# A new order for the items of phase one in a fused attention and MoE kernel

## The chip, the core and the metric

The kernel runs on one core of a Trainium2 chip. The metric is the device time of one execution in microseconds (us). Engines are named as in the profile: PE (TensorE matmul), PEld (its weight loads), DVE (VectorE), ACT (ScalarE), POOL (GpSimd), SP (SyncE, which here only issues transfers). L949 is line 949 of the kernel.

## The reference

Attention with pooled keys and values, followed by a feed-forward layer with a periodic activation, all in f32:

```python
# q, k, v: (8 batches, 8 heads, 576, 64)
k_p = k.reshape(B, H, 72, 8, D).mean(axis=3)
v_p = v.reshape(B, H, 72, 8, D).mean(axis=3)
scores = scale * np.matmul(q, k_p.transpose(0, 1, 3, 2))
scores = scores - np.max(scores, axis=-1, keepdims=True)
attn = np.exp(scores)
attn = attn / (np.sum(attn, axis=-1, keepdims=True) + 1e-09)
attn_out = np.matmul(attn, v_p)
x = attn_out.transpose(0, 2, 1, 3).reshape(4608, 512)
# w_in (512, 2048), w_out (2048, 512)
h = x @ w_in
s = np.sin(alpha * h)
g = h + s * s / (alpha + 1e-09)
out = g @ w_out
```

## The kernel before

**Two phases.** Phase one (to about 513 us) makes attention, `x @ w_in` and the activation, and stores g to a DRAM tensor, `g_bridge`. Phase two (`outputs`, matmuls of L1294) reads g back and multiplies by `w_out`. The change touches phase one only.

**Units and groups.** The tokens are cut into nine units of 512 and w_in into four column blocks, so that phase one has 36 groups, n = 4u + J (unit u, block J, here called group 0 to 3 of a unit). Each group makes a 2 x 2 block product with seven products in place of eight, `M1` to `M7`, of four matmuls each (`M5.2` is part 2 of the fifth, all of them L975). They need sums of blocks of x: `sums_of_x` (L939, items `sn`, `sx`) makes four of them per unit on DVE. In units 1 to 6 some products (5 and 1) are again split in seven smaller ones, with items `i.a`, `i.b`, `i.d`, `i.e` (matmuls, L1066) and the small copies and the add between them, `i.ca` (L1079), `i.cm`, `i.cb` and `i.ad` (L1089). These need sums made by `inner_x` (each unit) and `inner_w_in` (`w2_1`, `w2_5`; once, in unit 0), L931 on POOL.

**One group behind the products.** ACT and DVE bring the results from PSUM to the tile of g: `c16`, `p5`, `c67` are copies (L950), `a00`, `a01`, `a11`, `f10` DVE adds with a PSUM operand and `f1` one of SBUF tiles alone (all L949), `s` and `q` sine and square on ACT (L1044, L1051). `st` stores the tile of g with two transfers on SP's queue (L1099). The tile is called `h`; two buffers of it serve all groups in turn, so that the first write into a tile (the `a00` of a group) waits for the stores of the group two before. PSUM has eight banks: 0, 1, 2 and one of 3 and 4 in turn hold a group's accumulators; scores and `values` borrow from these and 5 to 7.

**Attention of the next batch.** In unit u, attention of batch u + 1 runs between the products: `scores`, the row maxima and their subtraction (`shift`), `exp`, `norm` (POOL, L496), `turn` (transposition on DVE) and `move` (transfers on SP), `values` (PE), and `out` (copies to x). Beside it the next inputs are loaded: `load_k`, `load_q`, `load_v` (six transfers on SP: two of L280, four of L285), pooled on POOL by `pool_k`, `pool_vm`, `pool_v`. `turn_q` turns q: `qa`, `qb`, `qc` on DVE, then `qd` and `qe` with eight transfers each on SP (L370).

**The order.** All these items stand in one agenda, each with a key; `perform` emits them in the order of the keys, and each engine keeps the order in which its instructions are emitted. A group adds 7 n to its keys, a unit 28 u:

```python
where = ORDER[self.kind(n)]
for m, f in acts.items():
    if m in where:
        self.at(7 * n + where[m], f)
```

`ORDER` (L42) is a table of such keys written out by hand: `U` for the attention items of units 1 to 6, `U0` for those of unit 0, `first0` to `first3` for the groups of unit 0, `enter` for the first group of unit 1, `mid0` to `mid3` for those of the units between, `exit` and `end0` to `end3` for the last ones. `F`, `U7` and `R` hold the start, unit 7's sums and later loads. Semaphores between engines follow from the tiles that an item reads and writes, so a new key changes what an instruction stands behind, never what it needs.

Of the kernel before, what the change touches and what calls it, by code (L numbers as in the profile page):

```python
# [43 lines left out]
    "load_k0": -3.59252, "load_v": -0.96965, "scores0": 3.279, "shift1": 6.66681, "shift0": 7.14828, "scores1": 7.66855, "shift2": 7.69635,  # L44
    "exp1": 11.39419, "exp0": 11.40344, "shift3": 11.6083, "exp2": 11.66391, "exp3": 11.68798, "norm0": 11.85811, "norm1": 11.86021, "norm2": 11.9294,
    "norm3": 11.93036, "pool_k0": 11.93266, "pool_v": 11.93269, "pool_vm": 11.9327, "turn2": 12.15533, "turn1": 12.33183, "turn3": 12.34767,
    "load_q": 13.4176, "load_k1": 13.54022, "turn0": 15.964, "move": 24.04575, "clean": 24.12855, "qa": 24.12869, "values": 24.12873,
    "out4": 24.12875, "qb": 24.12884, "pool_k1": 24.12885, "out0": 24.12885, "mark": 24.12895, "qc": 24.129, "out2": 24.129, "sx0": 24.1291,
    "inner_x": 24.12915, "out3": 24.33175, "k_t": 24.4364, "k_c": 24.4956, "qd": 24.83712, "out1": 24.87145, "sx1": 24.87995, "qe": 24.96216,
    "sx2": 25.5786, "sx3": 33.62096},  # L50
# [12 lines left out]
    "vsum": 1.50081, "qrest": 1.50141, "ahead": 1.502, "load_v": 2.08618, "pq0": 2.15962, "win3": 2.42169, "vals": 2.503, "sx2": 2.50351,  # L63
    "sx3": 2.50375, "score4": 2.504, "pq3": 2.82144, "win2": 2.94801, "pq4": 4.05233, "pq2": 4.0566, "pq1": 4.07221, "qt0": 4.511, "qt1": 4.51172,
    "kt0": 4.51227, "kc0": 4.96887, "scores0": 5.518, "shift0": 5.52, "shift1": 5.521, "comb1": 7.38091, "qt3": 7.92628, "qt2": 8.13953,
    "pool_vm": 8.75569, "qt4": 9.526, "exp1": 9.52613, "exp0": 9.52662, "scores1": 10.519, "shift2": 10.522, "norm0": 12.96627, "shift3": 13.00319,
    "comb2": 13.15659, "norm1": 13.38469, "turn0": 13.38824, "exp2": 14.22682, "exp3": 15.56789, "exp4": 15.57472, "load_k0": 16.01154,
    "load_q": 16.43872, "norm2": 16.65626, "load_k1": 16.66341, "norm3": 16.67159, "comb3a": 16.67343, "turn1": 16.69456, "comb3b": 16.77826,
    "turn3": 17.03674, "turn2": 17.289, "nrest": 17.37323, "move1": 18.86855, "move2": 18.96992, "clean": 18.98312, "move0": 19.548, "arest": 21.5955,
    "qc": 21.89678, "pool_v": 22.64595, "w2_1": 22.78383, "pool_k1": 22.83011, "pool_k0": 22.88021, "qa": 23.561, "qb": 23.562, "qd": 23.84216,  # L70
    "vrest": 26.13943, "values": 26.551, "qe": 26.565, "out0": 26.7312, "out2": 26.9598, "mark": 26.9713, "w2_5": 27.34755, "sn0": 27.5,
    "inner_x": 27.55453, "out1": 27.76959, "out4": 27.8955, "out3": 27.97572, "kt1": 28.19418, "sn2": 28.3493, "sn1": 28.40019, "kc1": 28.50762,
    "sn3": 28.51},
# [7 lines left out]
    "M1.2": -2.57294, "M1.0": -2.53472, "M1.1": -2.45741, "M1.3": -2.25355, "c16": -1.1367, "M5.0": -0.09345, "M5.1": 0.9728, "M2.0": 1.17425,  # L81
    "M6.0": 1.17485, "M2.1": 1.21724, "M6.2": 1.21765, "M5.2": 1.21779, "M6.1": 1.21784, "M6.3": 1.21789, "M5.3": 1.21819, "M2.2": 1.21845,
    "c67": 2.29615, "M2.3": 2.3555, "M7.0": 2.35565, "p5": 2.384, "s00": 2.38414, "q00": 2.3842, "M7.1": 2.5708, "M7.2": 2.57295, "M3.2": 3.16644,
    "M3.0": 3.47531, "M3.1": 3.63665, "M7.3": 3.7191, "M3.3": 4.06192, "a00": 6.599, "a11": 6.59915, "M4.0": 6.82409, "a01": 6.89334, "M4.1": 7.01225,
    "M4.2": 7.0125, "s11": 7.04685, "s01": 7.11736, "M4.3": 7.14095, "s10": 7.149, "q1": 7.19287, "q01": 7.22535, "f10": 8.3468, "f1": 8.63666,
    "st": 10.05},
"end1": {
    "M5.0": -3.33019, "M5.1": -2.72125, "M1.0": -0.17668, "M5.2": -0.17606, "M1.1": -0.17602, "M1.2": -0.06105, "M1.3": -0.0, "M5.3": 0.01245,
    "c16": 0.08171, "M6.1": 0.14395, "M6.0": 0.15524, "M6.2": 0.1611, "p5": 0.19815, "M6.3": 0.2009, "M2.1": 0.2077, "c67": 0.20789, "M2.2": 0.20881,
    "M2.3": 0.20922, "M2.0": 0.20955, "s00": 0.3, "q00": 0.3002, "a00": 2.19325, "M7.1": 2.79825, "M3.0": 2.80473, "M7.0": 2.81351, "M7.3": 2.88245,  # L90
    "M7.2": 2.88791, "M3.1": 2.88955, "M3.2": 2.9988, "M3.3": 3.21335, "a11": 3.46515, "s11": 4.32131, "M4.0": 4.4354, "a01": 5.1294, "M4.1": 7.91733,
    "M4.2": 7.92785, "M4.3": 7.99325, "s10": 8.1665, "q1": 8.17037, "s01": 8.2013, "q01": 8.36455, "f10": 9.25247, "f1": 9.6345, "st": 10.05},
"end2": {
    "M5.0": -5.21769, "M5.1": -4.19849, "M1.0": -3.17899, "M1.1": -2.75025, "M1.2": -2.51525, "M1.3": 0.90215, "M5.2": 0.99395, "M5.3": 0.99415,
    "c16": 1.14695, "p5": 1.1828, "M6.0": 1.4299, "M2.0": 1.4318, "M6.2": 1.43214, "M2.1": 1.43255, "M2.2": 1.5857, "M6.1": 1.71475, "M6.3": 1.7193,
    "M2.3": 1.7196, "c67": 1.78765, "s00": 1.78813, "q00": 1.79224, "M7.1": 2.3807, "M3.0": 2.38083, "M7.0": 2.38084, "M7.2": 2.38085, "M7.3": 2.3819,
    "a00": 2.69669, "a11": 2.7835, "M3.1": 3.71335, "M3.2": 3.93591, "M3.3": 5.35825, "M4.0": 5.57345, "a01": 5.76695, "M4.3": 6.28487,
    "M4.1": 6.46705, "M4.2": 7.97136, "s11": 9.31248, "s10": 9.36555, "q1": 9.36695, "s01": 9.43775, "q01": 9.4416, "f1": 9.6118, "f10": 9.90706,
    "st": 10.05},
"end3": {  # L100
    "M5.0": -5.29345, "M5.1": -4.88305, "M1.2": -2.23625, "M1.0": -1.54834, "M1.3": -1.48014, "M5.2": -1.2153, "M1.1": -1.21312, "c16": 2.27975,
    "M6.2": 2.3529, "M6.0": 2.35688, "M6.1": 2.35962, "M2.1": 2.36295, "M2.0": 2.3654, "M6.3": 2.3726, "c67": 2.37425, "M2.2": 2.4012,
    "M5.3": 2.40185, "M7.1": 2.41368, "M7.0": 2.41595, "M2.3": 2.4234, "p5": 2.48725, "M3.0": 2.51711, "M7.3": 2.5939, "M7.2": 2.61123, "a11": 2.612,
    "M3.1": 2.6266, "M3.2": 2.68157, "s00": 2.7151, "M3.3": 2.76182, "q00": 2.82195, "s11": 2.9428, "a01": 3.3439, "a00": 3.60325, "M4.1": 3.9026,
    "M4.2": 4.2433, "M4.0": 4.41961, "M4.3": 4.42479, "s01": 4.63625, "s10": 4.64555, "q01": 6.26891, "q1": 6.5869, "f1": 6.76776, "f10": 7.38579,
    "st": 10.05},
"enter": {
    "M1.0": -0.5012, "M1.2": -0.49378, "M1.1": -0.48667, "M1.3": -0.47146, "M5.0": -0.45225, "M5.1": -0.39509, "M5.2": -0.11055, "M5.3": -0.01999,
    "c16": 0.2794, "p5": 0.86945, "M6.0": 2.04465, "M2.0": 2.65792, "M2.1": 4.32577, "M2.3": 4.65506, "M6.1": 4.856, "M6.3": 4.86001, "M6.2": 4.87325,
    "M2.2": 6.26441, "c67": 7.13695, "s00": 7.13705, "q00": 7.13865, "a00": 9.0381, "M3.1": 9.2872, "M7.0": 10.26028, "M3.2": 11.00189,  # L110
    "M7.2": 11.0438, "M7.1": 11.12859, "M3.3": 11.34036, "M3.0": 11.34068, "M7.3": 11.41202, "a01": 11.61553, "a11": 11.72873, "M4.3": 11.78194,
    "M4.2": 11.92945, "s01": 11.93326, "s11": 11.9409, "M4.1": 11.9883, "M4.0": 12.04209, "s10": 12.24896, "q01": 12.24962, "q1": 13.17745,
    "f1": 13.21186, "f10": 13.40255, "st": 15.95645},
"exit": {
    "i.a": -5.02158, "i.ca": -4.768, "i.cm": -4.76115, "i.b": -4.15145, "i.cb": -3.5502, "i.d": -3.09985, "i.ad": -3.09835, "i.e1": -2.6215,
    "i.e5": -2.5921, "c16": -1.98745, "M6.3": -1.6521, "M6.1": 1.03682, "M2.1": 1.99737, "M6.2": 2.6094, "M2.0": 2.6097, "M6.0": 2.61059,
    "M2.2": 2.6107, "p5": 2.70895, "c67": 3.12873, "M2.3": 3.15565, "s00": 3.1652, "q00": 3.19285, "M3.1": 3.1934, "M7.0": 3.21229, "M3.0": 3.57143,
    "M7.3": 3.57944, "M7.1": 3.61026, "M7.2": 3.66851, "M3.3": 3.6861, "a00": 3.72485, "M3.2": 3.742, "a11": 3.8399, "a01": 4.32695, "M4.1": 4.53493,
    "M4.0": 4.5453, "M4.3": 4.82867, "M4.2": 4.96155, "s11": 5.86985, "s01": 5.87902, "s10": 5.9176, "q1": 6.17963, "q01": 6.2042, "f1": 6.79974,
    "f10": 7.5896, "st": 9.38135},  # L120
"first0": {
    "M1.0": 1.50081, "M1.3": 1.5013, "M1.2": 1.50138, "M1.1": 1.5016, "c16": 1.50164, "M5.2": 1.85931, "M5.3": 2.00457, "M5.0": 2.1577,
# [1448 lines left out]
```

## Time and profile before

| what | value |
|---|---|
| median of 3 runs | 905.83 us (905.42 to 906.15) |
| profiled execution, its span | 902.2 us |
| PE busy | 894.0 us, 99% |
| DVE busy | 678.2 us, 75% |
| ACT busy | 457.3 us, 51% |
| POOL busy | 206.5 us, 23% |
| granted PE clock, all slices | 9 of tenths (9 is 90% or more) |
| phase one, phase two | 0 to about 513 us, 513 to 902 us |

The profiled execution's own time is the span, 902.2 us; 3.6 us of the median lie around it. One unit takes 54.7 us, with the boundaries at about 86, 140.7, 195.4, 250.1, 304.8, 359.5 and 414.2 us. By such stretches the busy times are (us, with counts of instructions; then the granted clock, the share of the DMA engines and GB/s):

```profile
195.40:250.10 54.70, 54.70 (x470) 46.85 (x470) 37.85 (x65) 43.06 (x97) 23.40 (x29) 1.00 0.68 194
250.10:304.80 54.70, 54.70 (x471) 46.98 (x470) 38.01 (x65) 43.12 (x97) 23.56 (x29) 1.00 0.68 194
```

The columns after the stretch are its length, then PE, PEld, DVE, ACT and POOL. PE counts as busy through the whole of such a unit, while the other engines have from a fifth to more than a half of the time to spare.

### The profile page before, as it was taken

Reading aid. Unit: us, or ns where it says so; the run is one execution under the profiler, and the core shown is the slowest. Engines: PE = TensorE matmul, PEld = TensorE weight load, DVE = VectorE, ACT = ScalarE, POOL = GpSimd, SP = SyncE. Lnnn points to the kernel's source line nnn. Section 1 sums busy time; section 2 is a strip of 40 time slices with the busy share of each in tenths; the row PEclk is TensorE's granted clock in tenths of the full one; section 3 lists DMA queues with packets and bytes.
Section 4 is the critical chain, followed back from the end, with each engine's and each line's share of the span. In section 5 each row is a group of like instructions: output and inputs, shape, how many; then the busy total and the mean of one; then the engine's idle time right before and its main releaser. Section 6 shows DMA issues by size and latency. Waiting matters only on the chain.

```text
span 902.2 us, 18350 instructions
## 1 busy us (share of the span) xinstructions
PE 894.0 (99%) x7146; PEld 815.0 (90%) x7146; DVE 678.2 (75%) x1016; ACT 457.3 (51%) x1073; POOL 206.5 (23%) x235
## 2 busy tenths in 40 slices
PE   8999999999999999999999999999999999999997
PEld 5787888978888898888888899999999999999997
DVE  7576857668586684854466999979798888889894
ACT  5696878868787787786885611211111111111111
POOL 4969561814418164130000000000000000000000
PEclk9999999999999999999999999999999999999999
DMA  9956766666766666645426346261618172534401
GB/s 271 229 170 181 209 193 177 209 173 200 212 179 197 198 187 173 175 133 200 181 104 213 99 152 193 65 191 35 224 30 231 31 201 63 171 92 130 134 15 40
DMA packets 128751, 141.17 MB, mean 156 GB/s; under 512 B 46920, under 2 KB 95704, under 8 KB 128664
## 3 DMA queue, kind: packets, MB, share of 16 engines
q1 hardware_dynamic: 125880, 137.88, 52.6%
q10 hardware_dynamic: 2784, 2.11, 0.9%
q8 instruction: 57, 0.93, 0.4%
q14 instruction: 30, 0.25, 0.1%
HBM read 75.37 MB, written 47.19 MB: 136 GB/s over the span
## 4 chain that ended last, share of the span: by engine, by line
PE 98%; DVE 1%; DMA 0%; ACT 0%; issue 0%; ACTq 0%
PE PS L1294 43%; PE PS L975 41%; PE PS L1066 7%; PE PS L444 2%; PE PS L739 2%; PE PS L752 1%; DVE home L939 1%; DMA q<-in_q_dram 0%; PE PS L553 0%; PE PS L532 0%; PE PS L1131 0%; PE PS L416 0%; PE PS L697 0%; PE PS L343 0%; PE PS L695 0%; PE PS L607 0%
## 5 line engine op out<-in xcount | busy, mean ns | idle before, releaser
L975 PE MATMUL PS<-home,a 128*128 128x256 f32 x968 | 250.3, 382 | 0.0
L975 PEld LDWEIGHTS PS<-home,a 128*128 128x128 f32 x968 | 177.3, 190 | 28.6 <-issue 4.7
L975 PE MATMUL PS<-home,as 128*128 128x256 f32 x728 | 194.9, 381 | 0.9 <-DVE home L939 0.9
L975 PEld LDWEIGHTS PS<-home,as 128*128 128x128 f32 x728 | 134.1, 190 | 18.3 <-DVE home L939 0.9
L1294 PE MATMUL PS<-s,wb 128*128 128x144 f32 x896 | 119.1, 286 | 0.0
L1294 PEld LDWEIGHTS PS<-s,wb 128*128 128x128 f32 x896 | 113.6, 190 | 0.0
L1051 ACT ACTIVATE s<-s,c 128x256 f32<-128x256 f32 (+1 forms) x216 | 112.7, 580 | 0.0
L1344 POOL TENSOR_TENSOR cc<-cc,cb 128x576 f32<-128x576 f32 x1 | 2.0, 1974 | 483.1 <-DVE cb L1249 483.1
L949 DVE TENSOR_TENSOR h<-PS,s 128x512 f32<-128x512 f32 x72 | 49.5, 687 | 70.3 <-ACT s L1051 70.3
L1430 ACT COPY PS<-PS 128x144 f32<-128x144 f32 x56 | 14.7, 263 | 143.4 <-PE PS L1294 140.8
L1294 PE MATMUL PS<-r,wb 128*128 128x144 f32 x512 | 73.2, 286 | 0.0
L1294 PE MATMUL PS<-s,a 128*128 128x144 f32 x512 | 73.2, 286 | 0.0
L1044 ACT ACTIVATE s<-h,al 128x256 f32<-128x256 f32 x144 | 64.1, 502 | 16.4 <-DVE h L949 13.3
L271 POOL TENSOR_TENSOR kvin<-kvin 96x768 f32<-96x768 f32 (+3 forms) x42 | 69.9, 1665 | 3.1 <-DMA a<-in_moe_w_in_dram 0.6
L1294 PEld LDWEIGHTS PS<-r,wb 128*128 128x128 f32 x512 | 67.1, 190 | 0.1
L1294 PEld LDWEIGHTS PS<-s,a 128*128 128x128 f32 x512 | 67.1, 190 | 0.0
L949 DVE TENSOR_TENSOR h<-PS,p 128x512 f32<-128x512 f32 x72 | 49.1, 685 | 22.3 <-PE PS L975 21.7
L950 ACT COPY PS<-PS 128x512 f32<-128x512 f32 x72 | 41.4, 576 | 46.2 <-PE PS L975 23.0
L1044 ACT ACTIVATE s<-PS,al 128x256 f32<-128x256 f32 x144 | 60.3, 473 | 6.1 <-PE PS L975 5.8
L498 POOL TENSOR_TENSOR ex<-ex,sm 128x576 f32<-128x576 f32 (+1 forms) x28 | 35.2, 1270 | 109.8 <-DVE sm L497 108.9
L1412 ACT COPY PS<-PS 128x144 f32<-128x144 f32 x56 | 14.7, 263 | 88.7 <-PE PS L1294 88.7
L949 DVE TENSOR_TENSOR h<-h,s 128x1024 f32<-128x1024 f32 x36 | 44.8, 1246 | 14.2 <-ACT s L1051 14.1
(217 smaller groups left out, 1531.4 us busy)
## 6 DMA issues: line engine op xcount, KB each, us to landing
g_bridge<-h SPq DMA_DIRECT2D x72, 512.0 KB
r<-g_bridge SPq DMA_DIRECT2D x31, 1152.0 KB
out_dram<-o SPq DMA_DIRECT2D x122, 72.0 KB
kvin<-in_k_dram SPq DMA_DIRECT2D x14, 576.0 KB
q<-in_q_dram SPq DMA_DIRECT2D x7, 1024.0 KB
kvin<-in_v_dram SPq DMA_DIRECT2D x14, 512.0 KB
ex<-tr SPq DMA_DIRECT2D x54, 92.0 KB
ex<-tr SPq DMA_DIRECT2D x54, 88.0 KB
```

Of the source, the lines that this page charges most:

```text
L271: self.nc.gpsimd.tensor_tensor(out=t[..., 0:w] if w > D else out, in0=t[..., 0:w], in1=t[..., w:2 * w], op=OP.add)
L444: nc.tensor.matmul(ps[e][r0 + r:r0 + r + q.shape[-1], h, :], q[s], kb[s, hp, :], start=True, stop=True)
L498: nc.gpsimd.tensor_tensor(out=E(i), in0=E(i), in1=sm.unsqueeze(2).to_broadcast([P, n, Sp]), op=OP.mult)
L739: nc.tensor.matmul(o[r:r + 64], w, x, start=start and i < 2, stop=False, skip_group_check=True)
L949: add = lambda o, x, y: nc.vector.tensor_tensor(out=o, in0=x, in1=y, op=OP.add)
L950: copy = lambda o, x: nc.scalar.copy(out=o, in_=x)
L975: nc.tensor.matmul(ps[:, jj, :], self.A[p][:, kk, f * P:(f + 1) * P], x[:, kk, :], start=start and p not in G.begun, stop=(kk == 1), skip_ ...
L1044: self.nc.scalar.activation(out=G.s()[:, i, jj, j, :], in_=src[:, jj], func=AF.Sin, scale=self.al[:, f:f + 1])
L1051: self.nc.scalar.activation(out=x, in_=x, func=AF.Square, scale=self.c[:, f:f + 1])
L1066: nc.tensor.matmul(out, W[m][:, G.J], self.X2[p][m], start=start, stop=True, skip_group_check=True)
L1294: nc.tensor.matmul(out, W[:, J // 2, J % 2, :], A[:, J, :], start=(start and J == 0), stop=(J == self.NJ - 1), skip_group_check=True)
L1412: nc.scalar.copy(out=st["x1"][:, 1, :], in_=st["x1"][:, 0, :])
```

## The change

Only keys in `ORDER` are changed: in `U`, `U0`, `first0` to `first3`, `enter`, `mid0` to `mid3`, `exit` and `end0` to `end3`. `F`, `U7` and `R` stay, and no code beside the table is edited (it moves ten lines down, so that L949 before is L959 after; lines are named by their old numbers here). Every instruction, tile and transfer is the same in both kernels; only what stands before what on each engine differs. The keys of all loads stay as they were. Items on POOL and the DVE adds that read two SBUF tiles are placed so that they lie apart.

Many keys get new values with the same neighbours as before. Those that the prediction speaks of, in unit 0 (`U0`) and in units 1 to 6 (`U`, `mid2`), with all other keys left out:

```diff
 "U": {
-    "load_k0": -3.59252, "load_v": -0.96965, ...
-    "norm0": 11.85811, ... "pool_k0": 11.93266, "pool_v": 11.93269, "pool_vm": 11.9327, ...
-    ... "move": 24.04575, "clean": 24.12855, "qa": 24.12869, "values": 24.12873,
-    ... "qb": 24.12884, "pool_k1": 24.12885, ... "qc": 24.129, ...
-    "inner_x": 24.12915, ... "qd": 24.83712, ... "sx1": 24.87995, "qe": 24.96216,
+    "load_k0": -3.59252, "load_v": -0.96965, ...
+    ... "pool_v": 11.5152928, ... "norm0": 11.816381, ... "pool_k0": 12.3504188, ...
+    ... "pool_k1": 13.7954806, "turn0": 14.2914411, "move": 16.8183036, "pool_vm": 16.8469318,
+    "clean": 22.6818447, "qc": 22.6854708, "qa": 24.0974238, "values": 24.0975073, "qb": 24.1363647, ...
+    ... "inner_x": 24.3451414, ... "sx1": 24.5126011, "qd": 24.5236839, ... "qe": 24.532439,
 "U0": {
-    ... "pool_v": 22.64595, "w2_1": 22.78383, "pool_k1": 22.83011, "pool_k0": 22.88021, ...
-    ... "mark": 26.9713, "w2_5": 27.34755, "sn0": 27.5, "inner_x": 27.55453, ...
-    ... "kt1": 28.19418, "sn2": 28.3493, "sn1": 28.40019, "kc1": 28.50762, "sn3": 28.51},
+    ... "pool_v": 16.4275201, ... "pool_k1": 16.6636208, ... "w2_1": 24.4248686, ...
+    ... "sn0": 27.3094653, ... "pool_k0": 28.2511337, "sn1": 28.2512193, "sn2": 28.2512644,
+    "kt1": 28.2512817, "kc1": 29.1202333, "w2_5": 36.7683461, "inner_x": 36.9454661, "mark": 39.3525585, "sn3": 39.8922378},
 "mid2": {
-    "i.a": -2.3038, ... "f10": 10.1286, "s01": 10.12874, "q01": 10.88815, "f1": 11.0343, "st": 11.5035},
+    "i.a": -2.3730868, ... "f10": 10.0974848, "s01": 10.1335768, "q01": 10.5326811, "f1": 10.5635624, "st": 13.6858195},
```

## The prediction

> **What bounds the kernel now.** I read the page first, then the waits of PE, then the matmul starts of phase one, and only then the other engines' timelines, at the places where the new order moves something.
>
> ```profile
> PE 894.0 (99%) x7146; PEld 815.0 (90%) x7146; DVE 678.2 (75%) x1016; ACT 457.3 (51%) x1073; POOL 206.5 (23%) x235
> ```
>
> ```profile
> PE PS L1131 <- DVE full L1463: 1.1, 1, 1.1
> PE PS L532 <- DMA q<-in_q_dram: 1.0, 1, 1.0
> PE PS L975 <- DVE home L939: 0.9, 2, 0.5
> ```
>
> PE is busy 894.0 of 902.2 us, and the longest waits listed for it come to 3.0 us, 2.1 of them at the start, which the change leaves alone. Since a busy PE may hide stalls, I took the spacing of matmul starts in the trace. An L975 matmul follows the one before after 216 ns, an L1066 one after 112 ns. From about 30 us to 513 us nearly every start keeps this pitch. What exceeds it, other than the 0.1 us at each change between large and small tiles, is 1.3 us between 84 and 91 us and, in each 54.7 us unit, two places of 0.25 us where the last inner products wait for the add of L1089. Phase two, from 513 us, has no spare start at all and is not edited. So phase one's order can give back some 3 to 4 us and no more, while it can lose any amount: PE's work is the same, and only a new wait of PE makes a time.
>
> The adds that the change is about are those of L939 (`sums_of_x`), L949 with three SBUF tiles (`f1`) and L931 on POOL. Where they meet, this is seen; the timelines of DVE and POOL, start, us, instruction:
>
> ```profile
> 85.02 4.05 DVE L939 TENSOR_TENSOR home<-home 128x512 f32<-128x512 f32 x2 [1.68 <-ACT home L666]
> 89.00 1.75 DVE L939 TENSOR_TENSOR home<-home,home 128x512 f32<-128x512 f32 x1
> 91.09 1.34 DVE L939 TENSOR_TENSOR home<-home,home 128x512 f32<-128x512 f32 x1
> ```
>
> ```profile
> 86.93 1.59 POOL L931 TENSOR_TENSOR q<-q,as 128x512 f32<-128x512 f32 x1
> ```
>
> Four adds take 7.1 us beside `w2_5` (L931); with POOL idle one takes 0.69 us (the L939 add at 191.85 us).
>
> **The change, part by part.** Both kernels issue the same instructions; the sequences on each engine differ. I compared them item by item.
>
> (a) Boundary of units 0 and 1. `w2_5` (5 to 6 us on POOL) now follows `pool_k0`, ahead of `inner_x` and `mark`, and needs nothing that is late, so it ends near 84 us, before `sn0`. The four adds then cost 4 x 0.69 = 2.8 us. On PE that is worth what PE waits there: 0.71 + 0.15 us at 87 us (M5 of group 4 waits for `sn0`) and 0.49 us after `kt1`, together 1.3 us. Against it, SP now has unit 1's `load_k0` ahead of group 1's store, and group 2's store (1.07 us of SP) ahead of the last eight q DMAs, which feed `scores0` of unit 1 at 91.92 us; the last of them is issued at 89.1 us now, so up to 0.5 us can come back. I take 0.8 us gained, with bounds of 1.3 gained and 1 lost.
>
> [...]
>
> (b) In each unit one more matmul pair stands between the last `i.d` and `i.e` products of a group, so the two waits of 0.25 us go. The second of them is spent again: one M2 pair moves behind `values`, so `values` comes 0.43 us earlier after `i.e1`, while `p5`, which frees its bank, still ends behind the same ACT items. Net 0.25 us in 6 units: 1.5 us gained (bounds 0 and 3).
>
> (c) In units, `f1` meets POOL hardly at all (1.22 us mean, 1.54 us once), and the one add that does, `sx1` (0.95 against 0.69 us), stays beside `inner_x`. I cost this at nothing: M6, which waits for it, is 8 us later.
>
> (d) POOL: `pool_v` moves ahead of the norms, `pool_k1` ahead of `pool_vm`. `pool_v` waits for the v rows, which land before 268 us where norm0's multiplication stood at 269.5 us; `pool_vm` (5.4 us) would end near 292 us, `values` begins at 297 us. Covered by 1.5 us and 5 us. If that cover were gone, PE would wait at `values`.
>
> (e) SP: this is the one I find uncovered. SP's timeline at a boundary of units:
>
> ```profile
> 253.64 1.85 SPq L370 DMA_DIRECT2D q<-tr  x3
> 255.59 1.07 SPq L1099 DMA_DIRECT2D g_bridge<-h  x2
> 256.76 2.25 SPq L280 DMA_DIRECT2D kvin<-in_v_dram  x2
> 259.05 2.69 SPq L285 DMA_DIRECT2D vr<-in_v_dram  x4
> 267.89 0.96 SPq L1099 DMA_DIRECT2D g_bridge<-h  x2
> ```
>
> Sixteen q DMAs, the two stores of group 2 (`st`), the six v loads. `load_v` keeps its key, -0.97 from the next unit's start. Group 2 starts 14 keys before that start, so `mid2`'s `st` goes from 11.50 - 14 = -2.50 to 13.69 - 14 = -0.31. So the stores now stand behind the six loads. Queued behind them on SP is only group 3's store, 8 us later. Who waits is DVE: two `h` buffers serve all groups, and `a00` of the next unit's group 0 writes the buffer that these stores read; in the new sequence it waits for just these two landings. The same place on DVE, ACT and PE:
>
> ```profile
> 262.91 0.68 DVE L949 TENSOR_TENSOR h<-PS,s 128x512 f32<-128x512 f32 x1
> ```
>
> ```profile
> 263.91 0.36 ACT L1079 COPY PS<-PS 128x256 f32<-128x256 f32 x1
> ```
>
> ```profile
> 264.57 0.39 PE L1066 MATMUL PS<-ex,aM 128*128 128x128 f32 x2
> ```
>
> `a00` at 262.91 frees bank 1, `i.ca` copies into it, and `i.b` is the next product on it. From a landing to `i.b` take 0.68 + 0.36 + 0.1 us, so PE, which I place 0.25 us earlier by (b), waits for every landing after 264.57 - 0.25 - 1.15 = 263.2 us. Now the stores land at 261.71 (the last step of their semaphore in the trace's records): 1.2 us before they are needed.
>
> When would they land? The six loads take SP from 256.76 to 261.75, 5.0 us. The q DMAs can start earlier: they wait for DVE's `qa`, `qb`, `qc`, and `qc` (0.66 us) now precedes the two and waits only for moves that landed early; `qa` need no longer follow `f10`, but `qb` still does. That brings q's start from 244.98 to about 243.25, 1.7 us. So the stores are issued 3.3 us later, at 258.9. Fastest end: group 3's stores, with nothing in the queue, land 4.8 us after issue (267.89 to 272.67), which gives 263.7 and a wait of 0.5 us. Slowest end: the queue is served in order (the moves issued at 283.04, behind a store, send their first packet at 285.29, when the store's packets end). The v data took from 259.7 to 267.4 us, 7.7 us, of which the last 2.6 us were the `vr` loads, moving on about 4 of the 16 engines (24 packets of 86 ns in 0.5 us). In the new order the v data begin 1 us after their issue at 253.9 (as k loads do), so the four engines are free at 262.6; a store's share of 32 packets of 86 ns makes 265.4, and from the last packet to the landing 2.2 us passed before (259.5 to 261.71): 267.6 and a wait of 4.4 us. I am nearer to the slow end, since the order of the queue is seen and the four engines are seen, but the 2.2 us held other traffic; I take 266.0 us, a wait of 2.8 us.
>
> It occurs at the boundaries into units 2 to 6, five times (at the first the store comes before the loads, at the last there are no loads): 5 x 2.8 = 14 us, with bounds of 2.5 and 22. Nothing takes it back: DVE, ACT and PE stand together, and what follows in the unit shifts with them.
>
> [...]
>
> Sum: 905.8 - 0.8 - 1.5 + 14 = 917.5 us. The profiled span is 902.2, the runs' median 905.83, so 3.6 us lie around the span; the terms are differences and go on the median.
>
> **The rivals.** *The stores land in time* (faster). If the v loads leave the store's engines free early enough for a landing before 263.2 us, the change is left with (a) and (b): 905.8 - 2.3 = 903.5 us, at best 901. For it speaks that the fast end is only 0.5 us late; q's start would have to come 0.5 us earlier still, or the stores land in 4.3 us. Against it, the stores of this very place took 6.1 us (255.59 to 261.71) and the queue was in order. *Nothing reaches PE*: the adds are cleared but the 1.3 us returns by the q DMAs and (b) is lost to `p5`: 905.8. For it: 99% PE. *A wait at `values` instead*: `f10` of group 2 now stands between `qa` and `qb`, and frees the bank of `values`' second part. It waits with `qa` for the 15th move to land (near 239.8 us); if that comes 1 us late, PE waits 0.8 to 1.5 us in six units, 5 to 9 us, so 909 to 912 alone. Against it, `f10` waits until 241.4 us for its square already.
>
> **How the numbers follow.** Less than 0.2% (1.8 us) is no change for this kernel. Forecast (e): 0.71. Stores in time, 903.5: 0.17. Nothing: 0.07. `values`: 0.05, slower too. So faster 0.17, same 0.07, slower 0.76. The range takes the forecast's waits of up to 3.4 us (923) and reaches down to 903.5, where the first rival lies; outside are the slow end's last part (about 0.1) and the better half of that rival. The forecast's own range is 907 to 925.
>
> **What would show it.** Right: in the timeline of SP each group-2 store behind the v loads; on DVE an L949 `h<-PS,s` after 2 to 4 us of idle time put down to a DMA, five times, and as much idle or stretched time of PE before L1066; the unit period 57 instead of 54.7 us. The adds at 85 us near 0.7 to 0.9 us each. Wrong: a period of 54.5 us, or a00 at its old place behind the shifts, or PE waiting elsewhere.

## The result, and the profile after

The changed kernel takes 925.80 us (median of 5 runs, 924.61 to 927.17), the kernel before 905.83 us (5 runs, 905.42 to 906.22). The ratio is 1.0224, with a 95% interval of 1.0211 to 1.0236: 20 us slower. The forecast was 917.5 us in a range of 903.5 to 923: the right side, with a loss 8.3 us too small, and 2.8 us outside the range. All lines of the code stand ten lower in the changed kernel (L959 is the old L949). The profiled execution has a span of 925.4 us, and its own time is 927.17: 1.8 us lie around the span, and 1.7 to 2.1 in every execution that has both numbers. Other executions of the kernel before with a span of 902.2 us took 904.0 to 904.3 us, so the one profiled there was shorter than its kernel's median by some 1.7 us; the 3.6 us given above for the time around its span are too much by as much.

The page's first part and its chain, in the places of those of before:

```profile
PE 903.8 (98%) x7146; PEld 824.3 (89%) x7146; DVE 678.7 (73%) x1016; ACT 459.5 (50%) x1073; POOL 204.3 (22%) x235
```

```profile
PE 82%; DMA 7%; SPq 4%; DVE 3%; POOL 2%; issue 1%; ACT 1%; ACTq 0%; DVEq 0%; POOLq 0%
```

PE is busy for 98% of the span (99% before), and the span is 23 us longer. Of these, 2.3 us lie ahead of the first product, which starts at 23.9 us here and at 21.6 before. This start belongs to the execution and not to the order: over all the kernels below it lies at 21.4 to 21.9 us or at 23.0 to 23.9, whichever keys they have, while phase two takes 389.0 us in nearly all of them. What makes it early or late stays open; a difference of under some 2 us between two executions can be this start alone. The chain says more than the busy share: before, 98% of it was PE; now DMA and SP's queue hold 11%. The waits of PE and, below, of DVE (engine, line, what it waited for: us in total, times, longest):

```profile
PE PS L1076 <- ACT PS L1089: 10.4, 5, 3.3
PE PS L454 <- issue: 1.2, 1, 1.2
...
PE PS L732 <- DVE h L959: 0.9, 1, 0.9
PE PS L985 <- DVE h L959: 0.9, 1, 0.9
PE PS L749 <- DVE h L959: 0.3, 1, 0.3
```

```profile
DVE h L959 <- DMA g_bridge<-h: 14.6, 5, 3.8
```

Five waits of DVE for the landing of a store of g, and behind each, five waits of PE ahead of `i.b`. This is the place that step (e) of the prediction named. The boundary that the prediction showed now looks so, on SP, DVE, ACT and PE (start, us, instruction, idle time before it):

```profile
254.34 11.40 SPq L380 DMA_DIRECT2D q<-tr  x16
265.84 1.36 SPq L290 DMA_DIRECT2D kvin<-in_v_dram  x2
267.25 2.70 SPq L295 DMA_DIRECT2D vr<-in_v_dram  x4
270.06 0.90 SPq L1109 DMA_DIRECT2D g_bridge<-h  x2
```

```profile
278.37 0.69 DVE L959 TENSOR_TENSOR h<-PS,s 128x512 f32<-128x512 f32 x1 [2.41 <-DMA g_bridge<-h]
```

```profile
279.15 0.36 ACT L1089 COPY PS<-PS 128x256 f32<-128x256 f32 x1 [2.29 <-DVE h L959]
```

```profile
277.11 0.59 PE L985 MATMUL PS<-home,as 128*128 128x256 f32 x2
279.56 0.49 PE L1076 MATMUL PS<-ex,aM 128*128 128x128 f32 x2 [1.86 <-ACT PS L1089]
```

The second store is issued at 270.49 us and lands at 278.25 by its semaphore's records; `a00` starts 0.12 us later, and `i.b` 1.3 us after the landing.

**Where the 20 us are.** The pitch of a kind of matmul is the usual time from one start to the next (216 ns for L985). I added up by how much starts of matmuls exceed it, from the first product to the end of phase one, wherever it is over 0.15 us: 38.7 us after, 17.6 before (13.4 us of the latter and 15.3 of the former lie at `values`, where some starts lie far apart even without a wait: at 297.5 to 300.4 us of the kernel before by 371 to 374 ns at L739 and by 513 to 518 ns at L752). The 21.1 us between them, in this one execution: 11.2 us at the five `i.b`; 3.8 us of slow matmuls behind three of these; 1.9 us more at `values` of units 1 to 6 (15.3 against 13.4); 1.6 us more at the boundary of units 0 and 1 (5.4 against 3.8), where the granted clock is 0.50 from 86.07 to 89.48 us; 1.4 us inside the scores of unit 3, which the profile puts down to nothing that it shows ("issue"); 1.1 us at 60 us. The 3.8 us are seen in windows around the same wait (stretch, length, then busy us and instructions of PE, PEld, DVE, ACT, POOL, then PE's granted clock, DMA share, GB/s):

```profile
277.70:279.50 1.80, 0.01 (x1) 0.00 (x0) 1.13 (x2) 0.35 (x1) 0.46 (x1) 1.00 0.01 3
279.50:280.50 1.00, 0.94 (x6) 0.91 (x7) 0.97 (x2) 0.14 (x2) 0.00 (x0) 1.00 0.00 0
280.50:281.50 1.00, 1.00 (x4) 0.79 (x4) 1.00 (x2) 1.00 (x4) 0.00 (x0) 0.57 0.00 0
281.50:282.50 1.00, 1.00 (x5) 0.90 (x4) 0.67 (x3) 1.00 (x2) 0.00 (x0) 0.50 0.00 0
282.50:283.50 1.00, 1.00 (x4) 0.72 (x3) 1.00 (x1) 0.26 (x1) 0.00 (x0) 0.50 0.02 8
283.50:284.50 1.00, 1.00 (x6) 0.88 (x5) 0.97 (x4) 0.00 (x0) 0.00 (x0) 0.73 0.00 0
```

At 280.63 us, 1.1 us after PE is at work again, its clock falls to 0.5 for 3.41 us, and matmuls of L985 follow one another after 427 ns in place of 216.

### The profile page after: what moved, and what is told of

Read it like the earlier page. It is cut to its first block, busy times and chain, and to the rows that moved or that the text cites. A ratio compares the mean times of both kernels' runs of the same rounds, so it can differ in the third digit from the quotient of the medians.

```text
span 925.4 us, 18368 instructions
## 1 busy us (share of the span) xinstructions
PE 903.8 (98%) x7146; PEld 824.3 (89%) x7146; DVE 678.7 (73%) x1016; ACT 459.5 (50%) x1073; POOL 204.3 (22%) x235
## 4 chain that ended last, share of the span: by engine, by line
PE 82%; DMA 7%; SPq 4%; DVE 3%; POOL 2%; issue 1%; ACT 1%; ACTq 0%; DVEq 0%; POOLq 0%
PE PS L1304 42%; PE PS L985 30%; PE PS L1076 6%; DMA g_bridge<-h 4%; SPq L660 2%; PE PS L749 2%; DVE h L959 2%; DMA kvin<-in_v_dram 1%; DMA kvin<-in_k_dram 1%; PE PS L762 1%; POOL kvin L281 1%; SPq L380 1%; PE PS L454 0%; DMA a<-in_moe_w_in_dram 0%; PE PS L563 0%
## 5 line engine op out<-in xcount | busy, mean ns | idle before, releaser
L985 PE MATMUL PS<-home,a 128*128 128x256 f32 x968 | 253.0, 382 | 0.0
L985 PEld LDWEIGHTS PS<-home,a 128*128 128x128 f32 x968 | 178.1, 191 | 27.0 <-issue 5.5
L985 PE MATMUL PS<-home,as 128*128 128x256 f32 x728 | 197.2, 386 | 0.9 <-DVE h L959 0.9
L985 PEld LDWEIGHTS PS<-home,as 128*128 128x128 f32 x728 | 136.1, 193 | 18.7 <-DVE h L959 1.3
L959 DVE TENSOR_TENSOR h<-PS,s 128x512 f32<-128x512 f32 x72 | 49.0, 683 | 58.1 <-ACT s L1061 42.0
L281 POOL TENSOR_TENSOR kvin<-kvin 96x768 f32<-96x768 f32 (+3 forms) x42 | 66.9, 1594 | 25.7 <-DMA kvin<-in_k_dram 24.1
L1054 ACT ACTIVATE s<-h,al 128x256 f32<-128x256 f32 x144 | 65.2, 503 | 12.0 <-DVE h L959 11.7
L959 DVE TENSOR_TENSOR h<-h,s 128x1024 f32<-128x1024 f32 x36 | 50.5, 1402 | 25.4 <-ACT s L1061 24.6
L959 DVE TENSOR_TENSOR h<-PS,p 128x512 f32<-128x512 f32 x72 | 49.0, 687 | 24.1 <-PE PS L985 22.5
L1304 PE MATMUL PS<-x,wb 128*128 128x144 f32 x384 | 54.9, 286 | 0.0
```

Source lines behind the costliest of these rows:

```text
L281: self.nc.gpsimd.tensor_tensor(out=t[..., 0:w] if w > D else out, in0=t[..., 0:w], in1=t[..., w:2 * w], op=OP.add)
L959: add = lambda o, x, y: nc.vector.tensor_tensor(out=o, in0=x, in1=y, op=OP.add)
L985: nc.tensor.matmul(ps[:, jj, :], self.A[p][:, kk, f * P:(f + 1) * P], x[:, kk, :], start=start and p not in G.begun, stop=(kk == 1), skip_ ...
L1054: self.nc.scalar.activation(out=G.s()[:, i, jj, j, :], in_=src[:, jj], func=AF.Sin, scale=self.al[:, f:f + 1])
L1304: nc.tensor.matmul(out, W[:, J // 2, J % 2, :], A[:, J, :], start=(start and J == 0), stop=(J == self.NJ - 1), skip_group_check=True)
```

## The experiments

Each kernel ran in 5 rounds beside the kernel before on the same chip (905.3 to 905.6 us there). Intervals are of the ratio to the kernel before.

**1. `a_st`: the stores back ahead of the v loads, the rest of the change kept.**

```diff
 "mid2": {
-    ... "st": 13.6858195},
+    ... "st": 11.5035},
```

> The changed kernel with one key set back: `st` of `mid2` at 11.5035, so that group 2's stores stand ahead of the v loads again. Theory Q (the queue): the five waits of `a00` for the landing of these stores, 11.2 us of PE in the profile after, and the matmuls at a granted clock near 0.5 behind three of them, 3.8 us, are the one large cost; without them 925.8 - 15.0 = 910.8 us (909 to 913), and no L959 `h<-PS,s` waits over 1 us for `g_bridge<-h`. Theory W (the new order of DVE and ACT around `a00` and `i.ca` is itself late, and the landing only ends a wait that another instruction would end next): a gain under 5 us, 920 or more, with PE still waiting ahead of `i.b`.

Measured: 907.8 us (906.56 to 909.14), ratio 1.0030 (1.0018 to 1.0041). One key of several hundred holds 18.0 of the 20 us. No wait of DVE for `g_bridge<-h` and none of PE at `i.b` is left in the profile, and the granted clock is 1.00. Theory Q holds, theory W falls. The gain is 3 us above the 15.0 that I read from the one profile. The profile of this kernel also lacks the waits at 60 us (1.1 us) and in the scores (1.4 us) and the slow clock at 86 us (1.3 us of the boundary's starts). Waits at these two places are seen in other kernels with the same keys there (near 60 us in runs 7, 8 and 10, in the scores in run 5), and the execution profiled here is the shortest of its six (906.56 us), the one profiled after the change the longest of its five. So a part of the 3 us is the difference of executions; how it divides is not settled.

**2. `b_st`: the same key alone, put into the kernel before.**

```diff
 "mid2": {
-    ... "st": 11.5035},
+    ... "st": 13.6858195},
```

> The kernel before with one key changed: `st` of `mid2` at 13.6858, behind the v loads. Theory Q: in the old order q's transfers start later, the v loads end near 260.6 us and the stores are issued near 260.7; after the change stores issued behind the v loads landed 8.3 us and 8.8 us after issue (153.76 to 162.05, 212.76 to 221.53), which gives 269.0 to 269.5 against a need at 263.5: a wait of 5.5 to 6 us at five boundaries, 28 to 30 us, and the slow clock behind each, some 1.3 us: 935 to 942 us. If the landing follows DMA work that is over at the same time as in the changed kernel, 921. Theory W: 905.8, within 1 us.

Measured: 946.5 us (945.05 to 949.5), ratio 1.0461 (1.0442 to 1.0479): 41 us, above the expected 30 to 36. Its waits (lines as in the kernel before):

```profile
PE PS L1066 <- ACT PS L1079: 24.6, 5, 5.4
PE PS L975 <- ACT PS L950: 3.8, 4, 1.4
```

```profile
DVE h L949 <- DMA g_bridge<-h: 27.4, 5, 6.0
```

The five waits are 4.7 to 5.6 us each at `i.b`, 25.5 us by the starts, somewhat under the expected 28 to 30. Added to them are slow matmuls behind all five (8.8 us) and a new wait for a copy of ACT, 1.0 to 1.5 us, one group later in four of the units. Two things follow. The rest of the change softens its own mistake: its q transfers are earlier, so that the first v load is issued 10.3 us ahead of the need for the landing (the landing less PE's wait, mean of five boundaries) and here 7.4 us, and the waits are 1.2 to 3.5 us instead of about 5. And in both kernels, at all ten boundaries, the second store lands 2.49 to 2.51 us after the last v load, though 7.6 to 8.4 us after its issue: at these boundaries the landing goes with the end of the v data, not with the issue.

**3. `b_u0`: only unit 0's sections of the change in the kernel before** (`U0`, `first0` to `first3`, `enter`).

> The kernel before with only unit 0's keys of the change (`U0`, `first0` to `first3`, `enter`). What the two profiles show at the boundary of units 0 and 1 (starts beyond the pitch: 5.4 us after, 3.8 us before) and one wait of 1.1 us at 60 us belong to these keys: 905.8 + 2.7 = 908.5 us (907.5 to 910). The prediction's term (a) says 905.0 (904.5 to 906.8). If the later stretches lose because unit 0 hands them something late, more than 912.

Measured: 914.4 us, ratio 1.0104 (1.0091 to 1.0117). No theory gave this number. The profile shows new waits at 98 to 109 us (4.5 us: scores, a product, `i.b`), where the new `enter` meets the old `mid1`, 1.5 us at 60 us and 1.5 us at 184 us. Half of a new order set against half of an old one makes waits that neither whole order has, so this run says little on what unit 0's keys are worth in the change.

**4. `a_bu0`: the change with the stores ahead of the v loads, but unit 0 by the old keys.**

> The changed kernel with group 2's stores ahead of the v loads again (`st` of `mid2` at 11.5035) and the old keys for unit 0 (`U0`, `first0` to `first3`, `enter`): what is left is the change's order inside units 1 to 8. Theory Q: 925.8 - 15.0 - 2.7 = 908.1 us, and 905 to 907 if the extra starts beyond the pitch at `values` (1.9 us over six units) and at the scores of unit 3 (1.4 us) are followers of the stalls; 904.3 (the prediction's term (b), 1.5 us gained) if these are all. Theory W: 917 or more.

Measured: 909.1 us, ratio 1.0048 (1.0035 to 1.0061), by its number what Q gave, though not by its sum: 3.2 us of it are waits at 98 to 122 us, again where the two orders meet. So unit 0's old keys are no better beside the new units as they stand (909.1 against 907.8), but without these waits the kernel would be at 905.9 us, by my estimate: whether unit 0's new keys cost something, this run does not tell.

**5. `a_act`: the change, group 2's stores issued by ACT.**

```diff
-            self.nc.sync.dma_start(out=self.gd[i, ...
+            (self.nc.scalar if self.kind(Q.n) == "mid2" else self.nc.sync).dma_start(out=self.gd[i, ...
```

> The changed kernel with the two group-2 stores of units 1 to 6 (`mid2`) issued by ACT instead of SP, at the same key; the loads stay on SP. In the changed kernel a store issued behind the v loads landed 7.7 to 8.3 us after its issue and 2.5 us after the last v load landed, at all five boundaries; with `st` ahead of the v loads it landed 4.2 to 5.2 us after its issue. Theory Q (the stores wait for their turn in SP's queue): on a queue of their own they land 4 to 5.5 us after issue while the v data are still moving, `a00` waits less than 1 us, and the time is 925.8 - 15 = 911 us plus what two issues per unit cost ACT: 909 to 914. Rival E (the DMA engines themselves are full with v data, whichever queue): the stores land no sooner than 2 us after the v loads, waits of 1 to 3 us stay at most boundaries: 918 or more.

Measured: 910.9 us (907.32 to 911.72), ratio 1.0055 (1.0039 to 1.0071), within Q's 909 to 914. PE waits at no `i.b` in the profile, which is that of the shortest of the six executions (907.32 us); what makes the others longer, and the kernel 3 us slower than run 1, is not seen. The twelve stores stand on ACT's queue:

```profile
g_bridge<-h ACTq DMA_DIRECT2D x12, 512.0 KB
```

ACT issues them at about the time of the v loads, and they land 7.4 to 8.0 us later, yet 3.6 to 4.8 us before the last v load. So neither theory is whole: beside the v data the stores took longer than Q's 4 to 5.5 us, but on a queue of their own they did not land behind that data, as they did on SP by 2.5 us. ACT also issues them some 4 us earlier against the v loads than SP did, and this run does not part the two.

**6. `a_vr`: the change, the four `vr` loads behind the stores, the two large v loads ahead.**

```diff
+        def rest():
             for s in range(2):
                 for c in range(2):
                     ...
+        self.load_vr = rest        # agenda item "load_vr", key -0.25 in "U"
```

> The changed kernel with `load_v` cut in two: the two L280 loads (1 MB) at the old key, the four small `vr` loads behind group 2's stores. Theory Q with the vr loads as the last part of the turn: their data landed 2.4 us after the second L280 load's, so the stores are issued 2.7 us and land about 2.4 us earlier; the waits of 3.5, 1.2, 2.0, 2.9 and 1.6 us become 1.1, 0, 0, 0.5 and 0, and the slow clock behind them (3.8 us) goes: 925.8 - 9.6 - 3.8 = 912.4 us (910 to 915). Rival: what counts is the bytes ahead (0.26 of 1.3 MB are vr), a fifth of some 8 us = 1.6 us earlier: 925.8 - 7.6 - 2.5 = 915.7, 914 to 918.

Measured: 913.2 us (911.52 to 915.49), ratio 1.0091 (1.0076 to 1.0106). The time lies in the first theory's range. The landings seem to be the rival's: from the first v load's issue to the second store's landing 10.6 to 11.5 us, mean 11.05, against 12.3 to 13.0, mean 12.5, so 1.5 us earlier (the bytes gave 1.6, the other theory 2.4). But a landing is the last of sixteen steps of the store's semaphore, and the steps in the trace's records say otherwise. Counted from the first v load's issue, as means of the five boundaries, in the changed kernel the eleventh step comes after 10.1 us, the twelfth after 11.1, the fifteenth and the sixteenth after 12.5. Here the eleventh comes after 9.9 us, the fifteenth after 10.2 and the sixteenth alone after 11.05. Without the `vr` loads ahead of the store, then, the fifteenth step is 2.2 us earlier and the eleventh about where it was. In the changed kernel's last us of data, at the boundary shown (276.75 to 277.75 us), the trace has 48 packets of 84 ns, 4.0 us of packet time in 1 us: that of about four of the 16 engines, as an estimate. So the special weight that the prediction gave to the `vr` loads is borne out; what holds the landing in this run is one late step behind fifteen others. At four boundaries of five a 16 KB packet of the queue that the profile's page calls `instruction` starts 2.7 to 3.2 us ahead of that step and takes some 1.0 us; that it is the cause was not tried. PE's waits at `i.b` fall from 10.4 to 3.9 us by the list of waits.

**7. `a_sn`: run 1 with `w2_5` ahead of `pool_k0`, so that POOL works beside the adds of L939 again** (`"w2_5": 28.2`).

> The changed kernel with group 2's stores ahead of the v loads (907.8 us measured) and in unit 0 `w2_5` moved ahead of `pool_k0`, so that POOL's additions of L281 lie beside the four adds of L939 at 88 to 91 us, as POOL's work lay there in the kernel before. If these meetings are what unit 0's part of the change was worth: the adds take 1.3 to 4 us in place of 0.69 each, PE's M5 of group 4 waits for `sn0` by 0.5 to 1.3 us again, and the time is 908.3 to 909.3. Rival (DVE is ahead of PE there, the adds are not late): the adds are longer and PE shows no wait: 907.8, within 0.5.

Measured: 906.4 us (904.11 to 910.87, 12 runs), ratio 1.0021 (1.0008 to 1.0035). The meeting took place (DVE; POOL):

```profile
88.30 0.70 DVE L949 TENSOR_TENSOR home<-home 128x512 f32<-128x512 f32 x1 [1.66 <-ACT home L676]
89.41 1.82 DVE L949 TENSOR_TENSOR home<-home,home 128x512 f32<-128x512 f32 x1 [0.41 <-ACT home L676]
91.15 1.48 DVE L949 TENSOR_TENSOR home<-home 128x512 f32<-128x512 f32 x1
```

```profile
88.41 3.67 POOL L281 TENSOR_TENSOR kvin<-kvin 96x768 f32<-96x768 f32 x2
```

Beside POOL two of the adds take 1.82 and 1.48 us, in run 1 all take 0.69, and PE waits between 84 and 96 us in neither. The rival is right in what PE does: at this boundary, in the new order, the adds' meeting with POOL costs it nothing. The time is 1.4 us under the rival's 907.8, though nothing that PE waits for was taken away; so much can lie between two of these kernels without a cause that the profiles show. Its profile shows a wait of 1.6 us near 59 us, though, that run 1's does not:

```profile
58.40 0.71 DVE L640 STREAM_TRANSPOSE tr<-ex 128x512 f32<-128x512 f32 x1 [2.26 <-POOL ex L508]
```

**8. `a_val`: run 1 with `values` one pair of matmuls later** (`"values": 24.13` in `U`).

> The changed kernel with group 2's stores ahead of the v loads (907.8 us) and `values` of units 1 to 6 behind one more pair of M2 matmuls (key 24.13), 0.43 us later on PE. In two of six units PE waited 0.7 to 0.9 us at `values` for `p5` and restarted slowly (3.6 us of starts beyond the pitch in place of 2.2). If the pair that the change took from ahead of `values` is the cause: both waits shrink to below 0.5 us, 1.4 to 2.6 us gained, 905.2 to 906.4. If the release is late by more than 0.5 us or `out` becomes late behind it: 907.5 to 909.

Measured: 908.3 us (905.22 to 911.52, 12 runs), ratio 1.0035 (1.0020 to 1.0049): nothing gained against 907.8. The starts beyond the pitch at `values` fall from 15.9 to 14.5 us, but 0.7 us of waits for `out`'s copies appear behind them, and this execution has a 1.5 us stall by "issue". Moving the waiter was not the cure.

**9. `a_norm`: run 1 with unit 0's `pool_vm` behind `norm0`** (`"pool_vm": 9.6`).

> The changed kernel with group 2's stores ahead of the v loads (907.8 us) and, in unit 0, `pool_vm` behind `norm0` on POOL (key 9.6). In the changed order POOL's `comb2` waits for w_in's rows until 47.7 us, `pool_vm` (4.5 us) follows and `norm0` begins at 57.2 us where it began at 51.6; `turn0` on DVE waits 2.3 us for it, `a01` of group 1 stands behind `turn0`, and PE waits 1.0 to 1.7 us near 58 to 60 us. Theory P (POOL's new order is not covered in unit 0): the wait of `turn0` and that of PE go, 906.1 to 906.8. Rival (another step holds `a01`, or `pool_vm` is then late for `values_rest`): the wait stays or moves, 907.3 to 908.3.

Measured: 906.3 us (903.21 to 907.85, 11 runs), ratio 1.0013 (1.0002 to 1.0023), by its median theory P's gain. But the wait of `turn0` only became one of 3.0 us at the next `turn`, with 1.5 us of PE at 65 us, so the profile does not bear the median out. What stands ahead of it is w_in: POOL's `comb2`, now ahead of the norms, waits for these rows until 45.8 to 50.1 us in the executions seen.

**10. `a_qa`: run 1 with `qa` behind group 2's `f10` on DVE, as before the change** (`"qa": 24.09749`).

> The changed kernel with group 2's stores ahead of the v loads (907.8 us) and `qa` of units 1 to 6 behind `f10` of group 2 (key 24.09749), as before the change. The prediction's third rival said that `f10` behind `qa`, which waits for the last moves to land, frees `values`' bank late. Now DVE waits 2.6 us at `qa` for `ex<-tr`, and PE 0.3 us at `values` for the add, with slow starts behind it, in one of six units; in another it waits 0.7 us for `p5`. Theory R (the rival holds in part): the DVE-made waits at `values` go, 0.5 to 1.5 us gained, 906.3 to 907.3, and `values`' starts beyond the pitch fall from 3.5 to 2.3 us in that unit. Rival: only `p5` on ACT sets the start of `values`: 907.8, within 0.5.

Measured: 906.1 us (904.29 to 907.84, 11 runs), ratio 1.0011 (1.0003 to 1.0020), 1.7 us under run 1, as theory R said. By the time alone this is not clear of what two kernels can differ by (run 7 is 1.4 us under run 1, and the intervals of runs 1 and 10 overlap); the profile has to show it. What it removes, from run 1's DVE, is `f10` (L959) behind a `qa` that waits for the moves:

```profile
353.15 1.25 DVE L367 STREAM_TRANSPOSE tr<-q 128x1024 f32<-128x1024 f32 x1 [2.56 <-DMA ex<-tr]
354.32 0.65 DVE L959 TENSOR_TENSOR h<-PS,s 128x512 f32<-128x512 f32 x1
```

Without it `f10` comes 3.7 us after the add of L959 ahead of it in place of 5.0, and `values`' starts beyond the pitch fall to 13.6 us, the kernel before's 13.5. That is 2.3 us of starts in the one profile, over six units. The execution profiled also shows the worst case of run 9's matter:

```profile
DVE tr L640 <- POOL ex L508: 4.5, 1, 4.5
```

with 3.8 us of PE behind it.

**11 and 12. `a_best` and `a_best2`: the repairs together.** Both have `st` of `mid2` at 11.5035, `qa` at 24.09749 and `q00` of `first3` behind group 2's `q1` (3.4905). The first has `pool_vm` at 9.6, the second instead `comb2` behind `norm0`, as before the change (13.15659).

> The two edits above together, and `q00` of `first3` behind group 2's `q1` on ACT, which brings `f10` of group 2 0.9 us forward, for which `values_rest` waits 0.9 us at 82 us. If all three waits go: 907.8 - 1.3 - 1.0 - 1.1 = 904.4 us (903.5 to 905.5), under the kernel before (905.3). If the waits only move: 906.5 to 908.

> As the kernel with the two edits and `q00` behind `q1` (903.7 us), but with POOL's order in unit 0 as before the change at this place: `pool_vm` at its changed key first, then `norm0`, then `comb2` (key 13.15659), so that no `norm` of unit 0 stands behind the wait for w_in's rows, which ended between 46.8 and 50.1 us in the runs. Theory P (the waits of `turn` on DVE near 57 to 63 us come from that landing): DVE waits at most 1.1 us for `norm` as before the change, PE has no wait between 50 and 66 us in the profile, the runs spread less than from 901.7 to 908.4, and the median is 902.5 to 903.7, 0.2 to 0.3% under the kernel before (905.4). Rival (`comb2` then ends late for group 2's products): a wait of PE near 60 us, 904 to 906.

Measured: 903.7 us (901.69 to 908.37, 12 runs), ratio 0.9995 (0.9981 to 1.0009), and 903.95 us (902.31 to 905.9, 11 runs), ratio 0.9988 (0.9978 to 0.9998). The second is the only kernel here whose interval lies below the kernel before. It has no wait of PE between 50 and 66 us, DVE's wait there is

```profile
DVE tr L640 <- POOL ex L508: 0.6, 1, 0.6
```

and its runs spread over 3.6 us, not 6.7. So the new order, with four of its moves put right, comes out ahead by 1.5 us in the medians (0.2 to 2.0 by the interval), and by 1.5 us from the first product on in the two profiles (490.05 against 491.57 us to phase two); the prediction gave 2.3 us to (a) and (b).

## Why the prediction was wrong

The forecast added 14 us for (e) and took off 2.3 us for the rest, 11.7 us in all; measured are 20.0. Two steps failed: the sum has no term for the slow matmuls behind a wait (3.8 us), and the gains of (a) and (b) with the covers of (d) came out as a loss (4.5 us away from what was said). Against them stand waits that were 2.8 us shorter in all than forecast; some 3 us of what run 1 gained are left over, and their cause is open.

**(e), the stores behind the v loads: the mechanism right, its size 14 us instead of 18.** Place, order of events and count (five boundaries) were as said, and so was the way from landing to `i.b`: 1.3 us against 1.15. The waits themselves were 11.2 us, 2.24 each against 2.8. The landing came 12.5 us after the first v load's issue, where the prediction's numbers give 12.1 (253.9 to 266.0), but it was needed only 10.3 us after that issue, where they give 9.3 (253.9 to 263.2). That 266.0 came so near is luck in part: it was chosen between two ends, and the slow one, 267.6, rests on 2.2 us from a store's last packet to its landing, which took 0.4 us at all five boundaries (277.86 to 278.25). In the row that gave the 2.2 us, fifteen of the store's sixteen steps were in at 260.43 us and one alone came at 261.71. That the stores land behind the v data and that the last part of this data is slow were right: the landing came 2.49 to 2.51 us after the last v load (run 2), and the last us of data held 4.0 us of packet time, about four engines' (run 6). The cover that the stores had before is given as 1.2 us; by the prediction's own numbers (263.2 less 261.71) it is 1.5.

The term that was missing is what a wait of PE costs after it has ended: 3.8 us of matmuls at half clock behind three of the five waits (8.8 us behind all five in run 2). Phase one of the kernel before has no such wait, and I gave it no price. The slow end, 22 us, would have held the sum, but with waits that were not there.

**The rest of the change: +2.2 us instead of -2.3** (run 1 against the kernel before, interval 1.6 to 3.7). From the first product to phase two the two profiles differ by 0.8 us only (492.33 against 491.57), so how much of the 2.2 us is the order's is not settled; a gain it is not.
- (a), 0.8 us gained: the adds do take 0.69 us each (three at 91.70, 92.81 and 93.42 us) and PE's waits for `sn0` and behind `kt1` are gone, but PE now waits 0.9 us at `values_rest` for `f10` of group 2, and in the profile after the change (not in run 1's) the matmuls that follow run at half clock. In run 1 the boundary holds 4.1 us of starts beyond the pitch, before 3.8. A stall went to what was late next, and I had not asked for that.
- (b), 1.5 us gained: the waits for the add of L1089 are gone, but a unit of run 1 is only some 0.14 us shorter where nothing else delays it (54.60 and 54.57 us from one unit's first score matmul to the next's, before 54.75 and 54.71), 0.8 us over six, since 0.23 us of it returns at the start of `values`.
- (c), nothing: PE waits for no such add. But the adds are not all shorter, as was meant: `f1` takes 1402 ns on average after the change (L959, `h<-h,s`) and 1246 before.
- (d), POOL covered: wrong in unit 0. I checked `pool_v` and `pool_vm` against `values` and left out that `comb2` and `pool_vm` now stand ahead of `norm0`, whose reader `turn0` stands ahead of `a01` on DVE. The price is 0 to 3.8 us of PE from one execution to the next: none where `comb2` could start at 45.8 or 46.8 us (runs 5 and 1), 3.8 us where it started at 50.1 (run 10).

**The rivals.** The one at `values` (`f10` behind `qa`), to which I gave 5 to 9 us alone and a chance of 0.05, is real but small: 1.7 us by run 10's median, 2.3 us by the starts at `values`, neither far from what executions differ by. The two that ended at or under 905.8 us fell.

## What to carry to other kernels

When a queue's issue is moved, look first for the data that now stands ahead of it in that queue, and then for the writer that waits until its buffer has been read out; here one key moved past six loads cost nine tenths of the loss. Count a stall of PE with the slow matmuls that follow it (3.8 us here behind five waits of 11.2), and follow every stall that is removed to the wait that is next. On an order by hand, undo one key at a time before judging the rest: the remainder here needed three more keys to come out ahead, and its declared aim, keeping two engines' adds apart, was worth nothing at the one place where it was tried (run 7). And see which part of an execution a small difference lies in: here the start alone, which the change does not touch, varied by 2 us.

## What the runs showed of the hardware

- The times at which the granted clock fell lie on a grid of 3.413 us. In the changed kernel it falls to 0.5 at 86.07, 164.58, 280.63 and 338.66 us, each time for 3.41 us, and these times lie 23, 34 and 17 steps of 3.413 us apart (252.59 us in all); the five falls of run 2 lie 19, 19, 18 and 19 steps apart and last one or two steps. In the step ahead of a fall PE was idle for 1.86 us (277.22 to 280.63), 2.2 and 2.6 us (ahead of 164.58 and 338.66) and, among the short matmuls of `values`, for only 0.92 us (ahead of 86.07). Steps with 0.92 us (58.77 to 62.18), 1.10 us (157.75 to 161.17) and 1.20 us (215.78 to 219.19) had no fall behind them, nor had the waits of 1.0 and 1.5 us. In run 6 a wait of 3.2 us was divided by the grid (counted back from the clock's fall at its end, at 911.51 us) into 1.4 and 1.8 us, and the clock stayed at 1.00:

```profile
157.16:160.58 3.42, 2.04 (x12) 1.51 (x10) 0.29 (x1) 1.19 (x2) 0.00 (x0) 1.00 0.74 281
160.58:163.99 3.41, 1.62 (x10) 1.52 (x11) 2.78 (x4) 1.17 (x4) 1.32 (x3) 1.00 0.09 33
```

  So the length of a wait alone does not part these cases: one of 1.86 us within a step had a fall behind it, one of 3.2 us across two steps had none. How much of it lies in one step does so for these waits (1.86 to 2.6 us with a fall behind it, at most 1.8 us without); the two steps with 0.92 us, one with a fall behind it and one without, show that idle time is not the whole of it.
- On SP's queue, the second store behind the v loads landed 2.50 us after the last of them, within 0.01 us at ten boundaries of two kernels (the changed one and run 2). At these boundaries the last four of the store's sixteen steps come 2.0 to 2.7 us after the eleventh; with the small loads moved behind the stores the fifteenth comes 0.3 us after it and the sixteenth 1.15 us, as means (run 6). Issued on ACT's queue, at the time of the loads, the stores landed 3.6 to 4.8 us ahead of the last of them (run 5).
- Beside DVE's add `f1` of two SBUF tiles (83.47 us, 1.38 us long), POOL's L941 add of 83.85 us took 2.15 us in run 7; the seven others of its size at 77.47 to 87.18 us took 1.27 or 1.28 us.
- Some of the kernels spread more than the kernel before: 6.3 to 6.8 us between the extremes in runs 7, 8 and 11, against 2.6 to 2.8. The landing of w_in's rows, 45.8 to 50.1 us, and the start (the first product at 21.4 to 23.9 us) are two things that vary; that they are the whole cause was not tried.
- The stalls of 0.4 to 2.3 us that the profile calls "issue" (scores of unit 3 in three of the kernels) go with packets of the `instruction` queue: of seven such stalls of over 0.8 us by the starts, in five kernels, six end 1.2 to 1.5 us after the end of a 16 KB packet of this queue (in the changed kernel the packet ends at 216.93 us and PE starts again at 218.23), the seventh 0.4 us after one. That the packet is the cause was not tried.
